# Windowed attention with a gated feed-forward on one core: distance bias on TensorE and a different weave in the first two halves

## The chip, the cores and the metric

The kernel runs on one NeuronCore of a Trainium2 chip. The core has five engines that run side by side, each through its own list of instructions in order: PE (TensorE, matrix multiplies), DVE (VectorE), ACT (ScalarE), POOL (GpSimd) and SP (SyncE, which here only issues DMAs). POOL issues DMAs too. All DMAs share the core's 16 DMA engines. The metric is the device time of one execution in microseconds (us), as the median of several runs; lower is better.

## The reference

Attention over 4 batches, 8 heads, 768 positions and a head width of 64, followed by a feed-forward on the concatenated heads (3072 tokens of width 512, inner width 1536):

```python
scores = scale * np.matmul(q, k.transpose(0, 1, 3, 2))
is_global = pos[None, :] < n_global            # 8 global keys
is_local = (rel >= 0) & (rel < n_local)        # the last 96 keys
dist = np.where(is_global & ~is_local, float(n_local), np.abs(rel))
scores = scores - slopes[:, None, None] * dist[None, :, :]
scores = np.where(is_global | is_local, scores, -1e9)
x = softmax(scores) @ v                        # then heads side by side: 3072 x 512
out = (np.maximum(x @ w_gate, 0.0) * (x @ w_val)) @ w_out
```

All inputs and the output are fp32; the kernel computes in bf16 and accumulates in fp32.

## The kernel before

**Halves.** The work is cut into eight halves s = 0 to 7: half of one batch, 384 query tokens each. Every half has an attention part and a feed-forward part (called c, with the same number). A half's 384 tokens lie on 128 partitions, three tokens each (`NN = 3`).

**Attention of a half.** Heads are handled in four pairs p. Keys are cut into seven tiles of 120 local keys, and the eight global keys are put in front of each tile, so that a tile has 128 rows; only the pieces of the score matrix inside the window are computed. For halves 0 and 1, `piece_cast` turns fp32 q and k of a pair into bf16, `piece_t` transposes them on PE (six 128x128 transposes into PSUM) and copies them out on DVE to `qT` (one copy per head, L259 and L260) and to `kT` (`put_keys`, L238 to L244). For halves 2 to 7 the same is done ahead of time by POOL casts (`kc`, `qz`), DMA transposes on SP (L275, L279) and POOL copies (`early_pieces`); this is called the preparation of a half below. `piece_qk` computes scores for both heads of a pair with one matmul per key tile: the query operand is block-structured, with the other head's 64 rows zero. ACT takes the exponential out of PSUM (L309), and DVE multiplies it by `m_all`, the exponential of the biased distance, which is zero outside the window (L318). `m_all` is made at the start by eight ACT instructions (L209) from the distances `dd`, which POOL and DVE build (L177 to L201). `piece_av` (halves 2 to 7) multiplies by v with a block of ones beside it, so that sums and products come out together; `piece_av_wide` (halves 0 and 1) does sums and products in separate matmuls. ACT then forms the reciprocal as exp(-ln) (`lnd`, `rcp`), and DVE writes the normalised result to `xT` (L351, L377).

**Feed-forward of a half.** `ffn_pieces(c)` gives two lists. f1 has 24 items: for each of 12 slices of 128 inner columns a gate item (four matmuls L408, ReLU on ACT L411) and a val item (four matmuls L418, product on DVE L420 into `ht`). f2 has six items of six matmuls (L427), two for each 128 output rows, then a copy on ACT (L432) and an output DMA on SP (L433). Weights come in three groups of four slices, each group a gate and a val load on POOL's queue (`load_w_group`); `wo_sb` holds the output weights.

**Order.** The order of instructions on each engine is the order in which the Python code issues them. `weave` walks through the feed-forward items and puts attention items between them at given fractions of their total estimated cost. The stages before are:

1. attention of half 0 alone, with loads placed in it by hand (the table `aside`)
2. the first eight items of f1 of half 0, with attention of half 1 spread over them and past their end
3. the first eight items of f1 of half 1
4. the second groups of both halves, with the preparation of half 2
5. the third groups of both halves and both f2 lists, with attention of half 2 and the preparation of half 3
6. then, for c = 2 to 7, f1 and f2 of half c with attention of half c+1 and the preparation of half c+2

The loads of q and k of halves 1 and 2 are held back by `load_qk_after`: DVE writes one element of the target tile, so that the loads, on SP's queue, wait for DVE to get there (L158).

```python
    weave(f1_0[G[0]], spread(attention_pieces(1), 0.1, 1.6),
          [(0.9, lambda: load_w_group(2)), (0.95, lambda: load_w(wo_sb, moe_w_out, 0, DM))])
    ...
    load_qk_after(2)
    load_v_half(2)
    weave(f1_1[G[0]])
    weave(f1_0[G[1]] + f1_1[G[1]], spread(early_pieces(2), 0.0, 1.0),
```

**Buffers.** PSUM has eight banks: three for scores and transposes (`qk_ps`), two for attention output (`av_ps`), three for the feed-forward (`ff_ps`).

Of the kernel before, what the change touches and what calls it, by code (L numbers as in the profile page):

```python
# [8 lines left out]
FP32 = mybir.dt.float32  # L9
# [6 lines left out]
def kernel(  # L16
# [12 lines left out]
    nc = tc.nc  # L29
# [18 lines left out]
    BIG = 1.0e5  # L48
# [13 lines left out]
    banks_of_half[1] = [[by[1, 2], by[1, 5]], [by[1, 3], by[1, 6]], [by[1, 4]]]  # L62

# [4 lines left out]
    es_pool = ctx.enter_context(tc.tile_pool(name="es", bufs=3))  # L68
# [6 lines left out]
    qk_psum = ctx.enter_context(tc.tile_pool(name="qkps", bufs=3, space=bass.MemoryType.PSUM))  # L75
    av_psum = ctx.enter_context(tc.tile_pool(name="avps", bufs=2, space=bass.MemoryType.PSUM))
    ff_psum = ctx.enter_context(tc.tile_pool(name="ffps", bufs=3, space=bass.MemoryType.PSUM))
# [17 lines left out]
    m_all = const.tile([128, H, 2, NN, WQ], BF16)  # L95

# [66 lines left out]
    for p in range(HP):  # L163
        load_qk(0, 2 * p, 2 * p + 2)
    zeros = setupp.tile([128, QH], BF16)
    nc.vector.memset(ident, 0.0)
    nc.vector.memset(zeros, 0.0)
    nc.vector.memset(ones, 1.0)


    dd = setupp.tile([128, 2, NN, WQ], FP32)
    pos = setupp.tile([NG, NN, WQ], FP32)
    relg = setupp.tile([NG, NN, WQ], FP32)
    rel = setupp.tile([128, NN, WQ], FP32)
    sel = setupp.tile([128, NN, WQ], FP32)
    half_w = KT - 0.5
    nc.gpsimd.iota(pos, [[2, NN], [2 * NN, WQ]], base=-(2 * NL + KT - 3), channel_multiplier=0,  # L177
                   allow_small_or_imprecise_dtypes=True)
    nc.gpsimd.iota(relg, [[2, NN], [2 * NN, WQ]], base=-(NL - 1), channel_multiplier=-2,
                   allow_small_or_imprecise_dtypes=True)  # L180
# [8 lines left out]
    nc.gpsimd.affine_select(out=ident, in_=ident, compare_op=ALU.not_equal,  # L189
                            fill=1.0, base=0, pattern=[[-1, 128]],  # L190
                            channel_multiplier=1)
    ga = setupp.tile([NG, NN, WQ], FP32)
    gd = setupp.tile([NG, NN, WQ], FP32)
    nc.vector.tensor_mul(ga, pos, pos)
    nc.vector.tensor_scalar(ga, ga, half_w * half_w, 1.0, op0=ALU.is_gt, op1=ALU.mult)
    nc.vector.tensor_mul(gd, relg, relg)
    nc.vector.tensor_scalar(gd, gd, (NL - 0.5) ** 2, 1.0, op0=ALU.is_lt, op1=ALU.mult)
    nc.vector.scalar_tensor_tensor(out=gd, in0=pos, scalar=half_w, in1=gd,
# [3 lines left out]
    def zero_q(i, p):  # L202
        nc.scalar.copy(qTb[i][64:128, p, 0, :], zeros[64:128])
        nc.scalar.copy(qTb[i][0:64, p, 1, :], zeros[0:64])
# [269 lines left out]
    for i, (_, f) in enumerate(a0):  # L474
        for g in aside.get(i, []):
            g()
# [79 lines left out]
```

The softmax here doesn't subtract the row's maximum and nothing guards it: scores larger than these inputs give would overflow.

## Time and profile before

| what | value |
|---|---|
| median of 5 runs | 258.49 us (257.95 to 260.27) |
| the profiled execution's own time | 260.27 us |
| its span (first to last instruction) | 258.5 us |
| PE busy | 236.5 us (91%) |
| ACT busy | 158.9 us (61%) |
| DVE busy | 139.6 us (54%) |
| POOL busy | 93.0 us (36%) |
| mean granted PE clock | 0.993 |
| first feed-forward matmul begins | 23.69 us |
| last matmul of attention of half 1 | 43.1 us |
| first feed-forward matmul of half 2 begins | 89.8 us |

The span is counted from the first instruction of the profiled execution; 1.77 us of its time lie outside. An engine that is busy for the whole of a stretch sets its length; where no engine is, waits between engines or transfers do. The times of matmuls overlap, so the busy time of PE is read from its start times. Stage boundaries are read from the first start of the matmuls of a stage in the timeline of PE.

### The profile page before, as it was taken

To read this page: it belongs to the slowest core of one execution; us is meant where nothing else is said; L and a number is where in the kernel's file an instruction comes from. 1 tells how busy PE (TensorE), PEld (TensorE's weight loads), DVE (VectorE), ACT (ScalarE), POOL (GpSimd) and SP (SyncE) were. 2 spreads that over 40 slices of the span, in tenths; PEclk is the share of its full clock that TensorE was granted. 3 is DMA by queue.
4 is the path that set the end of the run, shared out by engine and by line. 5 is a ranking of instruction groups with operands and counts; after the bars stand their busy time and mean duration, and the time that the engine had idled before them with its cause. 6 is when DMAs were issued, how large, how long until landed. Compare 5 with 4: busy or idle time off the path is not lost.

```text
span 258.5 us, 4684 instructions
## 1 busy us (share of the span) xinstructions
PE 236.5 (91%) x1599; PEld 138.9 (54%) x1608; DVE 139.6 (54%) x369; ACT 158.9 (61%) x321; POOL 93.0 (36%) x232
## 2 busy tenths in 40 slices
PE   1567698999999999999999999999999999999994
PEld 0335364666555566655665566655565566556641
DVE  7775786464644456534675276625663457614410
ACT  8757277333567577756775577747774677643311
POOL 8951796066544706700644335600640000000000
PEclk9999899999999999999999999999999999999999
DMA  6999699956996994684670984924661200021012
GB/s 181 196 191 234 161 189 205 244 128 144 267 84 176 191 266 112 138 88 148 198 154 13 186 263 104 124 84 144 185 145 42 81 3 0 0 81 43 0 41 82
DMA packets 82695, 34.35 MB, mean 133 GB/s; under 512 B 58608, under 2 KB 79600, under 8 KB 82672
## 3 DMA queue, kind: packets, MB, share of 16 engines
q1 hardware_dynamic: 50816, 26.16, 37.1%
q0 software_dynamic: 31856, 7.91, 31.0%
q8 instruction: 12, 0.20, 0.3%
q14 instruction: 11, 0.09, 0.1%
HBM read 28.38 MB, written 6.29 MB: 134 GB/s over the span
## 4 chain that ended last, share of the span: by engine, by line
PE 79%; DVE 9%; DMA 4%; ACT 4%; issue 1%; SPq 1%; POOL 0%; ACTq 0%; DVEq 0%
PE ff_ps L427 23%; PE ff_ps L418 22%; PE ff_ps L408 22%; PE qk_ps L306 5%; PE av_ps L334 5%; DMA qs<-in_q_dram 4%; DVE xT L351 2%; PE qk_ps L254 1%; DVE ht L420 1%; DVE es L318 1%; ACT lnd L343 1%; DVE qk L223 1%; ACT rcp L348 1%; DVE kT L238 1%; ACT lnd L372 1%
## 5 line engine op out<-in xcount | busy, mean ns | idle before, releaser
L408 PE MATMUL ff_ps<-xT,wg 128*128 128x384 bf16 x384 | 79.0, 328 | 0.4 <-DVE xT L377 0.2
L418 PE MATMUL ff_ps<-xT,wv 128*128 128x384 bf16 x384 | 78.6, 327 | 0.6 <-DVE ht L420 0.3
L411 ACT ACTIVATE grelu<-ff_ps 128x384 bf16<-128x384 f32 x96 | 47.1, 490 | 38.9 <-DVE ht L420 21.8
L420 DVE TENSOR_TENSOR ht<-ff_ps,grelu 128x384 bf16<-128x384 f32 x96 | 53.2, 554 | 28.0 <-PE ff_ps L418 23.6
L427 PE MATMUL ff_ps<-wo_sb,ht 128*128 128x512 bf16 x279 | 66.3, 379 | 0.5
L309 ACT ACTIVATE es<-qk_ps 128x432 bf16<-128x432 f32 (+2 forms) x96 | 49.4, 528 | 19.4 <-PE qk_ps L306 17.3
L318 DVE TENSOR_TENSOR es<-es,m_all 128x432 bf16<-128x432 bf16 (+6 forms) x144 | 42.1, 329 | 23.4 <-ACT es L309 22.9
L351 DVE TENSOR_TENSOR xT<-av_ps,rcp 64x384 bf16<-64x384 f32 x48 | 26.6, 555 | 46.3 <-ACT rcp L348 41.7
L418 PEld LDWEIGHTS <-wv 128*128 128x128 bf16 x384 | 36.6, 98 | 24.4 <-issue 3.4
L408 PEld LDWEIGHTS <-wg 128*128 128x128 bf16 x384 | 36.5, 98 | 23.3 <-issue 0.5
L427 PEld LDWEIGHTS <-ht 128*128 128x128 bf16 x288 | 26.9, 97 | 27.8
L306 PE MATMUL qk_ps<-qT,kT 128*128 128x432 bf16 (+6 forms) x144 | 34.1, 308 | 1.3 <-ACT es L309 1.3
L264 POOL CAST kc<-ks 128x384 bf16<-128x384 f32 x24 | 11.7, 530 | 58.5 <-DMA ks<-in_k_dram 49.0
L343 ACT ACTIVATE lnd<-av_ps 64x384 f32<-64x384 f32 x48 | 23.3, 485 | 11.0 <-PE av_ps L334 10.4
L432 ACT COPY osb<-ff_ps 128x512 f32<-128x512 f32 x24 | 14.1, 586 | 24.4 <-PE ff_ps L427 23.5
L129 POOL DMA_DIRECT2D vbuf<-in_v_dram x28 | 24.4, 878 | 0.8 <-issue 0.4
L334 PEld LDWEIGHTS <-vbuf 128*128 128x128 bf16 x216 | 18.1, 98 | 8.2 <-issue 0.7
L334 PE MATMUL av_ps<-es,vbuf 128*128 128x216 bf16 (+4 forms) x216 | 21.1, 226 | 0.5 <-DVE xT L351 0.5
L306 PEld LDWEIGHTS <-kT 128*128 128x128 bf16 x144 | 14.5, 103 | 12.0 <-issue 3.3
L254 PE MATMUL qk_ps<-ident,qk 128*128 128x128 bf16 x48 | 5.3, 265 | 12.3 <-DVE qk L223 8.3
L272 POOL CAST qz<-qs 128x192 bf16<-128x192 f32 x48 | 14.8, 359 | 2.3 <-DMA qs<-in_q_dram 2.2
L348 ACT ACTIVATE rcp<-lnd 128x384 f32<-128x384 f32 x24 | 12.5, 522 | 0.8
(68 smaller groups left out, 110.5 us busy)
## 6 DMA issues: line engine op xcount, KB each, us to landing
out_dram<-osb SPq DMA_DIRECT2D x24, 256.0 KB
ks<-in_k_dram SPq DMA_DIRECT2D x6, 768.0 KB
qs<-in_q_dram SPq DMA_DIRECT2D x6, 768.0 KB
vbuf<-in_v_dram POOLq DMA_DIRECT2D x24, 120.0 KB, 5.7
ks<-in_k_dram SPq DMA_DIRECT2D x8, 192.0 KB
qs<-in_q_dram SPq DMA_DIRECT2D x8, 192.0 KB
wg<-in_moe_w_gate_dram POOLq DMA_DIRECT2D x3, 512.0 KB, 7.3
wv<-in_moe_w_val_dram POOLq DMA_DIRECT2D x3, 512.0 KB, 9.0
```

The lines of the kernel that those rows point to most:

```text
L129: nc.gpsimd.dma_start(out=v_dst(b, NG + r0, NG + r0 + n, j), in_=v[b, :, KT * j + r0 : KT * j + r0 + n, :].rearrange("h p d -> p h d"))
L306: nc.tensor.matmul(ps[:, c : c + n_], lhsT=kt[:, j, :], rhs=qd[:, :, :, a : a + w], start=True, stop=True)
L309: nc.scalar.activation(es[:, 0:cols], ps[:, 0:cols], AF.Exp, bias=0.0, scale=scale)
L318: nc.vector.tensor_mul(e4, e4, mk)
L334: nc.tensor.matmul(av3[:, :, a : a + w], lhsT=vb[:, j, z0 : z0 + 128], rhs=es[:, c : c + NN * w].rearrange("k (n p) -> k n p", n=NN), star ...
L343: nc.scalar.activation(ln[o0 : o0 + 64], av[d0 : d0 + 64, 0:QH], AF.Ln, bias=0.0, scale=1.0)
L351: nc.vector.tensor_tensor(xT_of[s][r, p, :], av_of[s, p, e_][r, 0:QH], rc[r], op=ALU.mult)
L408: nc.tensor.matmul(psg[:, 0:QH], lhsT=w_of(wg, dc, fc), rhs=xT[:, dc, :], start=(dc == 0), stop=(dc == N_DC - 1))
L411: nc.scalar.activation(gr, psg[:, 0:QH], AF.Relu, bias=0.0, scale=1.0)
L418: nc.tensor.matmul(psv[:, 0:QH], lhsT=w_of(wv, dc, fc), rhs=xT[:, dc, :], start=(dc == 0), stop=(dc == N_DC - 1))
L420: nc.vector.tensor_tensor(ht[:, fc, :], psv[:, 0:QH], st["gr"], op=ALU.mult)
L427: nc.tensor.matmul(ps2, lhsT=ht[:, fc, n * 128 : (n + 1) * 128], rhs=wo_sb[:, fc, :], start=(fc == 0), stop=(fc == N_FC - 1))
```

## The change

In attention of half 0 the window and distance are no longer a factor after the exponential. PE first writes the bias into PSUM (`piece_bias`: a scaled identity `sid` of the head times the distance tile `dd`), then adds the scores (`piece_score`): one matmul per head and key tile that uses only the 64 rows of that head, so that `qT` of half 0 needs no zero blocks and is copied out once. The exponential covers two banks, both heads at once. The PSUM tiles of this part are three of two banks each; they are given back before the feed-forward, which then takes its own (`other_pools`). Transposes move to the `av_ps` banks. `dd` and `BIG` become bf16 values, and the global rows of `dd` are built by POOL instead of DVE.

Seven matmuls on zeros (`warm`) stand at the front of PE's list. The casts of half 0 are spread: pair 0 on DVE, pairs 1 and 2 on ACT, pair 3 on POOL. The eight `m_all` instructions move into the feed-forward that follows. On POOL's queue the loads of v and weights of the first group come after the distances, with the cast of pair 3 between them; the second weight group is issued after the casts of pairs 0 and 1 of half 1, the third after pairs 2 and 3.

The whole f1 list of half 0 (24 items instead of 8) is then woven with attention of half 1, with places given by hand, and half 1 now uses `piece_av`. Then follow f1 of half 1 with the preparation of half 2, and both f2 lists with attention of half 2 and the preparation of half 3. From c = 2 on the order is as before.

```diff
+    first_groups = [[by[0, 0], by[0, 1]], [by[0, 2], by[0, 3]]]
...
-    qk_psum = ctx.enter_context(tc.tile_pool(name="qkps", bufs=3, space=bass.MemoryType.PSUM))
     av_psum = ctx.enter_context(tc.tile_pool(name="avps", bufs=2, space=bass.MemoryType.PSUM))
-    ff_psum = ctx.enter_context(tc.tile_pool(name="ffps", bufs=3, space=bass.MemoryType.PSUM))
+    P["es"] = first.enter_context(tc.tile_pool(name="es2", bufs=4))
+    P["qk"] = first.enter_context(tc.tile_pool(name="qkps2", bufs=3, space=bass.MemoryType.PSUM))
+    def other_pools():
+        first.close()
+        P["es"] = ctx.enter_context(tc.tile_pool(name="es", bufs=3, reuse_waits="tile"))
...
+    nc.vector.memset(wo_sb[:, 0, :], 0.0)
...
+            nc.tensor.matmul(warm_ps, lhsT=wo_sb[:, 0, 0:128], rhs=wo_sb[:, 0, :], start=True, stop=True)
+    warm(7)
...
     for h in range(H):
+        nc.scalar.activation(sid[:, h], ident, AF.Copy, bias=0.0, scale=-slopes[h] / scale)
+
+    def mask(h):
         nc.scalar.activation(m_all[:, h], dd, AF.Exp, bias=0.0, scale=-slopes[h])
...
-            eng = nc.vector if s == 0 else nc.gpsimd
-            eng.tensor_copy(
+            copy = nc.gpsimd.tensor_copy
+            if s == 0 and p < 3:
+                copy = (nc.vector.tensor_copy, nc.scalar.copy, nc.scalar.copy)[p]
...
-        qd = qTb[s % 2][:, p]
-        nc.vector.tensor_copy(qd[0:64, 0, :], tp[0:64, 0, :])
-        nc.vector.tensor_copy(qd[64:128, 1, :], tp[64:128, 0, :])
+        if s == 0:
+            nc.vector.tensor_copy(qTb[0][:, p, 0, :], tp[:, 0, :])
...
+    def piece_bias(p, g):
+        ps = P["qk"].tile([128, 2, 512], FP32, name="qk_ps")
...
+                nc.tensor.matmul(ps[:, e, c : c + NN * w], lhsT=sid[:, 2 * p + e],
+                                 rhs=dd[:, 0 if j == 0 else 1, :, m : m + w],
+                                 start=(i == 0), stop=False, skip_group_check=True)
...
+    def piece_score(p, g):
...
+                r = slice(64 * e, 64 * e + 64)
+                nc.tensor.matmul(ps[:, e, c : c + NN * w], lhsT=kt[r, j, :],
+                                 rhs=qd[r, :, a : a + w], start=False, stop=(i == len(group) - 1),
+                                 skip_group_check=True)
...
+        nc.scalar.activation(es, ps[:, :, 0:cols], AF.Exp, bias=0.0, scale=scale)
...
         if s == 0:
-            return (C(0) + T(0) + C(1) + T(1) + QK(0) + C(2) + T(2) + QK(1) + C(3) + T(3) + QK(2) + AW(0)
-                    + QK(3) + AW(1) + AW(2) + AW(3))
+            return (C(0) + X(lambda: load_v_globals(0), lambda: load_v(0, 0)) + C(3)
+                    + X(lambda: load_v(0, 1), lambda: load_v(0, 2), lambda: spread_v_globals(0, 1, 4),
+                        lambda: load_v(0, 3), lambda: load_w_group(0))
+                    + C(1) + T(0) + BI(0, 0, 1) + C(2) + T(1) + SC(0, 0, 1) + BI(1, 0) + SC(1, 0) + T(2)
+                    + BI(1, 1) + SC(1, 1) + BI(2, 0) + T(3) + SC(2, 0) + BI(2, 1) + SC(2, 1)
+                    + BI(3, 0) + SC(3, 0) + BI(3, 1) + SC(3, 1)
+                    + AW(0) + X(lambda: load_qk_after(1, True)) + AW(1) + AW(2) + AW(3) + X(other_pools))
         if s == 1:
...
+            return ([(0.0, lambda: C_(0)), (0.0, lambda: C_(1)), (0.02, lambda: load_w_group(1)),
+                     (0.04, lambda: C_(2)), (0.05, lambda: C_(3)), (0.07, lambda: load_w_group(2))]
+                    + [(0.08, lambda j=j: fill_ones(nc.gpsimd, 0, j)) for j in range(NT)]
+                    + [(t, lambda p=p: piece_t(1, p)) for p, t in enumerate((0.10, 0.14, 0.20, 0.26))]
...
-    weave(f1_0[G[0]], spread(attention_pieces(1), 0.1, 1.6),
-          [(0.9, lambda: load_w_group(2)), (0.95, lambda: load_w(wo_sb, moe_w_out, 0, DM))])
+    weave(f1_0, attention_pieces(1),
+          [(0.05 * h, lambda h=h: mask(h)) for h in range(H)])
...
+    load_w(wo_sb, moe_w_out, 0, DM)
...
-    weave(f1_1[G[0]])
-    weave(f1_0[G[1]] + f1_1[G[1]], spread(early_pieces(2), 0.0, 1.0),
-          [(0.1 + 0.12 * j, lambda j=j: fill_ones(nc.vector, 0, j)) for j in range(NT)])
+    weave(f1_1, spread(early_pieces(2), 0.0, 1.0))
...
-    weave(f1_0[G[2]] + f1_1[G[2]] + f2_0 + f2_1,
-          spread(attention_pieces(2), 0.3, 0.9), spread(early_pieces(3), 0.4, 0.8))
+    weave(f2_0 + f2_1, spread(attention_pieces(2), 0.0, 0.9), spread(early_pieces(3), 0.2, 0.7))
```

## The prediction

> **What bounds the kernel now.** I read the span in slices first, then the stretches between the stage boundaries, the waits of PE, and the queues of POOL and SP.
>
> ```profile
> PE   1567698999999999999999999999999999999994
> POOL 8951796066544706700644335600640000000000
> DMA  6999699956996994684670984924661200021012
> ...
> PE 79%; DVE 9%; DMA 4%; ACT 4%; issue 1%; SPq 1%; POOL 0%; ACTq 0%; DVEq 0%
> ```
>
> One slice is 6.46 us. From the eighth on PE is at its limit; only the first seven, 43 us, have room. The stretches, cut at the stage boundaries (columns: stretch and length; busy time and count of PE, weight loads, DVE, ACT, POOL; granted clock; DMA share; GB/s):
>
> ```profile
> 0.00:23.69 23.69, 11.16 (x104) 7.11 (x105) 16.91 (x63) 18.02 (x37) 15.85 (x36) 1.00 1.33 197
> 23.69:43.06 19.37, 15.52 (x160) 9.39 (x157) 14.46 (x48) 11.55 (x25) 15.65 (x33) 0.91 1.01 189
> 43.06:89.98 46.92, 46.08 (x281) 26.23 (x282) 23.05 (x54) 24.13 (x50) 22.22 (x56) 1.00 1.00 177
> 89.98:118.45 28.47, 28.32 (x192) 16.93 (x192) 15.74 (x41) 19.65 (x39) 9.95 (x27) 1.00 0.77 151
> ```
>
> By 43.06 only eight f1 items are done (four matmuls each start 0.65 us apart as a group: 5.2 us) besides two attentions. From 43.06 on PE is 98% busy. So a gain can come only from the first two rows, and what counts is when c = 2 begins, 89.98; the remaining 168.5 us I leave as they are. Why PE starves there:
>
> ```profile
> PE qk_ps L254 <- DVE qk L223: 8.3, 3, 4.3
> PE qk_ps L254 <- POOL qk L223: 2.3, 1, 2.3
> ...
> 24.49 0.51 POOL L223 CAST qk<-qs 128x384 bf16<-128x384 f32 x1 [1.30 <-DMA qs<-in_q_dram]
> ...
> 28.28 0.51 POOL L223 CAST qk<-qs 128x384 bf16<-128x384 f32 x1 [1.10 <-DMA qs<-in_q_dram]
> ```
>
> In half 0 transposes wait for DVE's casts, since DVE does casts, copies and mask products in one row (transposes at 4.33, 7.36, 11.50, 15.45). In half 1 they wait for q and k from memory. A third loss follows from the second (rows as above):
>
> ```profile
> 26.46:29.87 3.41, 1.12 (x12) 0.77 (x12) 1.54 (x7) 0.49 (x1) 2.10 (x5) 1.00 0.67 210
> 29.87:33.28 3.41, 3.41 (x14) 1.73 (x13) 3.00 (x10) 1.94 (x4) 3.41 (x9) 0.50 0.68 90
> 19.63:23.04 3.41, 2.08 (x43) 1.66 (x42) 2.33 (x7) 3.08 (x8) 0.35 (x1) 1.00 1.19 231
> ```
>
> After 3.41 us in which PE was busy for 1.12, the clock is halved for 3.41 us, which loses 1.7 us of work; after 2.08 it was not.
>
> **What the Trainium skill says.** "TensorE: Matmul & The Clock Gate" (Part 1: The HAM clock gate) describes this: full clock after about 3.4 us of work, half after such an idle window. The trace agrees (six transposes take 0.82 us until 15.45, 0.50 from 25.40). The same page (Part 3: Packing small matmuls) says matmuls on separate row groups run side by side; no run here shows it. "DMA: Bandwidth & Descriptors" (Issuing engines are not separate DMA queues) says transfers of all issuers share 16 engines and interleave. The trace agrees with weights (19 to 22 us: 0.42 MB from POOL's queue, 0.27 MB from SP's), not with v: q and k of half 2, issued at 43.92, moved nothing to speak of until 48, while v moved (45.5 to 47.5: 0.30 MB, all POOL's).
>
> **Step 1, half 0.** Casts of pair 0 ran at 3.63 and 3.91, close behind their data, so the first transposes stay at 4.3. DVE loses ga/gd (2.6 us), six casts, 16 mask products (4 us) and one copy per pair; per pair it keeps 0.35 + 0.53 + 0.17 + 0.18 = 1.25 us. ACT takes over: eight `sid` (about 0.2 each, shorter than the 0.49 of 384 columns), four casts (0.49), then per pair exponentials of 864 and 336 columns: by the 0.0008 us per column between 384 and 512 columns, 0.89 + 0.45 = 1.34. ACT can start them after its casts, 7.4, and ends at about 13.8; then 4 x (0.49 + 0.52) for ln and exp. POOL's distance chain ends near 5.0 instead of 2.8, so v globals and tile 0 are issued by 6.9, the cast of pair 3 (its data arrive at about 8) runs until 8.8, and v tiles 1 to 3 are issued by 11.6; alone on the engines they need about 3.7 us from issue to landing (5.7 before, beside q and k): 14.6. That is the wait that replaces DVE's: the products of pair 0 wait for it, with the rest of PE's list behind. xT of pair 0 is done at 15.7 and, at ACT's 1.01 us per pair, of pair 3 at 19.05. Gate 0 ends at 19.7, against 24.9.
> Not shown before: 32 bias matmuls, 4 x 1200 columns, 0.5 us per pair at full clock, 1.0 at half. Bounds: below zero no, since they only add work; 0 behind ACT's 1.34 per pair, 2 us if the clock stays low. I take 0. Scores in row halves: 0.5 (side by side) or 1.0 per pair, both under 1.34: 0. Seven warming matmuls of 0.43 lie in the wait before 4.3: 0 to +0.3; their gain is contained in "full clock by about 8"; without it up to 1.7 us are lost.
>
> **Step 2, transfers.** The first weight group is issued at 11.6 instead of 7.76; 0.5 MB takes 2.6 us alone (landings at 35.0 and 37.6 before). wg lands at 18, wv, sharing with q and k of half 1, at 21.2. q and k (issued 15.75; before 15.45) are no longer beside the second group: alone they move at 350 GB/s, 0.6 us per transfer. Pair 0 is cast at 23.0, pair 1 at 24.7, pair 2 at 27.2, pair 3 at 28.2; transposes at 23.1, 24.8, 27.3, 29.2 (before 25.4 to 36.5). With val 0 waiting for wv until 21.2, eight items and all transposes are done at 30.4. The second group is now behind two casts on POOL, 24.7 instead of 14.87: it lands at 31.2 and 33.1, so gate 4 waits 0.7 and val 4 1.05. The third is issued at 28.2, lands by 38.5 and is needed at 40: hidden. `wo_sb` moves from 32.0 to 35.4, behind seven memsets more (2 us) on POOL: hidden, as f2 is far.
>
> **Step 3, the weave.** Left on PE at 30.4: 16 items x 0.65 = 10.4, eight score groups x 0.2 = 1.6, eight products x 0.3 = 2.4, waits 1.75: 46.5. From 25.3 ACT has 19.6 us (12 exponentials, five masks, ten ReLUs, eight ln, four exp), DVE from 25.5 18.9 us: until 45. Three engines almost full lose something to each other; I take 1.0 (0 to 3.5). f1 of half 0 ends at 47.5. Before, the same work was done at 43.06 + 10.4 = 53.5.
>
> **Step 4, preparation of half 2.** f1 of half 1: 15.6 + 0.3 for the last xT; the first f2 item ends at 64.7. Next on PE are scores of half 2. Their q and k are released by DVE at the end of f1 of half 0, 48.7.
>
> ```profile
> 43.92 0.37 SPq L110 DMA_DIRECT2D ks<-in_k_dram  x1
> 44.34 0.65 SPq L110 DMA_DIRECT2D qs<-in_q_dram  x1
> 46.80 6.17 SPq L125 DMA_DIRECT2D vbuf<-vbuf  x6
> 54.35 4.72 SPq L275 DMA_TRANSPOSE kN<-kc  x3
> 59.24 3.94 SPq L279 DMA_TRANSPOSE qT<-qz  x3
> ```
>
> Before, 43.92 to the landing of the last transpose, about 64.5, was 20.6 us, covered by 23.5 us until the first scores at 67.47. Now the cover is 16. From the k data on, the chain is 12 us (POOL 1.9, SP 4.7 + 3.9, landing 1.3) and stays. Only the data can be quicker: 4.1 us of the 20.6 were v tiles ahead; `wo_sb` now ends near 46, v near 50, so about 1.3 to 2 us of waiting remain. Ready at 65.9; PE waits 1.2.
>
> **Step 5.** Rest of f2: 11 x 1.3 = 14.3, attention of half 2 4.9, waits 0.4 as before: c = 2 begins at 85.5. The preparation of half 3 ends near 84.3, just ahead. 89.98 - 85.5 = 4.5 us. Against the profiled execution's 260.27 (span 258.5 and 1.77 around it) that is 255.8; its time is 1.78 above the median, so against the median 258.49 it is 254.0.
>
> **Rivals.** **A, main:** 254.0, own range 252.5 to 256.5, chance 0.50. **B, fewer waits:** weights and half 2 arrive just in time, no loss between engines: f1 ends at 45.0, half 2 without a wait: 7.7 us, 250.8. For it: DMA had idle time at 28 to 30. Against: four transfers are issued late. Chance 0.17. **C, ACT and DVE bound the weave:** 19.6 us of ACT work in 22 us, in fixed order: f1 ends at 50, 256.5. For it: the masks moved there. Chance 0.20. That the change does not do what it says, the clock staying low through half 0, costs 1 to 1.7 us and falls here. **D, slower: half 2 is late.** q and k of half 2 wait 6 us behind `wo_sb` and v (4.1 before), ready at 71.3: PE stands 6.6 us instead of 1.2 and the clock is halved after it, 1.7 more: 7.1 us worse than A, 261.1. It decides from 5.7 us of wait and clock together. For it: SP and POOL do this chain one after the other. Against: wo's issue moves by 3.4 us only. Chance 0.13.
>
> **The numbers.** A measurement of this kernel can tell about 0.5% from no change, 1.3 us: faster is below 257.2. Of A nearly all (0.48), B, and two thirds of C (0.13): 0.78; rests of A and C and the mild end of D: 0.10; D: 0.12. Range 250.5 to 259.5: it reaches from B to the near side of D and leaves out most of D and a better B.
>
> **What would show it.** First gate near 19; transposes of half 1 between 23 and 30; a wait of gate 4 for weights; c = 2 near 85.5; PE idle before the first scores of half 2 for 0 to 3 us. Wrong: a wait there above 5 us, a halved clock after 20, or f1 of half 0 ending after 51.

## The result and the profile after

The changed kernel takes 259.83 us (median of 43 runs, 258.89 to 262.28), the kernel before 258.83 (80 runs, 257.55 to 261.67) beside it. The ratio is 1.0037 (95% interval 1.0024 to 1.005): no gain, but a loss of 0.2 to 0.5%. The forecast was 254.0, with 0.78 on faster. The profiled execution took 259.35 us, its span is 257.6.

Beside the span in slices of 6.44 us stands the chain of work that ended last; this is the page of the kernel after:

```profile
PE   7744988999898899999999999999999999999994
PEclk9996799999999999999999999999999999999999
DMA  6999999994899993855682985937581200021012
...
PE 66%; DMA 16%; DVE 5%; ACT 4%; SPq 4%; POOL 2%; issue 2%; DVEq 0%; ACTq 0%; POOLq 0%
```

The first two slices are fuller than before (77 for 15), the third and fourth emptier (44 for 67), and the fourth and fifth ran at a low clock. In the chain the share of PE fell from 79% to 66% and that of DMA rose from 4% to 16%: the end is now reached by way of transfers. The stretches of the kernel after, cut at the last `xT` of half 0, the end of f1 of half 0, the begin of f2 and the last matmul of the first gate of c = 2 (columns as in the prediction):

```profile
0.00:19.65 19.65, 12.66 (x159) 7.92 (x159) 8.31 (x31) 13.54 (x29) 15.93 (x38) 1.00 1.01 150
19.65:50.02 30.37, 25.06 (x180) 15.79 (x181) 18.96 (x57) 20.73 (x44) 19.76 (x43) 0.89 1.31 199
50.02:66.28 16.26, 15.99 (x98) 9.38 (x97) 7.80 (x17) 5.89 (x13) 6.73 (x22) 1.00 0.87 174
66.28:89.59 23.31, 20.75 (x121) 10.67 (x123) 10.78 (x25) 14.50 (x31) 15.23 (x35) 1.00 1.20 212
```

Half 0 is done at 19.65, some 4 us earlier than before. Then 30.4 us pass until f1 of half 0 ends, where the forecast had 28.4 (19.05 to 47.5). What PE waits for there, in the timeline of PE of the kernel after (start, length, instruction, and in brackets the idle time ahead of it and what ended it):

```profile
20.25 0.82 PE L478 MATMUL ff_ps<-xT,wg 128*128 128x384 bf16 x4 [2.98 <-DMA wg<-in_moe_w_gate_dram]
23.79 1.46 PE L488 MATMUL ff_ps<-xT,wv 128*128 128x384 bf16 x4 [2.71 <-DMA wv<-in_moe_w_val_dram]
35.71 0.82 PE L488 MATMUL ff_ps<-xT,wv 128*128 128x384 bf16 x4 [1.23 <-DMA wv<-in_moe_w_val_dram]
68.36 0.53 PE L355 MATMUL qk_ps<-qT,kT 128*128 128x432 bf16 x2 [0.63 <-DMA qT<-qz]
81.36 0.42 PE L383 MATMUL av_ps<-es,vbuf 128*128 128x216 bf16 x4 [0.96 <-DVE xT L400]
89.59 0.32 PE L478 MATMUL ff_ps<-xT,wg 128*128 128x384 bf16 x1 [0.77 <-DVE xT L400]
```

Gate 0, val 0 and val 4 (the first val item on the second weight group) all wait for weights. Why these are late is in POOL's queue and in what the DMA engines moved meanwhile. POOL in the kernel after:

```profile
8.13 0.50 POOL L236 CAST qk<-ks 128x384 bf16<-128x384 f32 x1 [1.17 <-DMA ks<-in_k_dram]
9.23 2.70 POOL L141 DMA_DIRECT2D vbuf<-in_v_dram  x3
11.92 0.79 POOL L158 DMA_DIRECT2D wg<-in_moe_w_gate_dram  x1
24.36 0.51 POOL L236 CAST qk<-qs 128x384 bf16<-128x384 f32 x1 [0.66 <-DMA qs<-in_q_dram]
26.70 0.79 POOL L158 DMA_DIRECT2D wg<-in_moe_w_gate_dram  x1
```

The transfers between 8 and 16 us, in slices of 0.2 us, first of the kernel before and then of the kernel after:

```profile
DMA  9999999999999999999999999999999999999999
...
DMA packets 5099, 1.50 MB, mean 187 GB/s; under 512 B 4098, under 2 KB 5099, under 8 KB 5099
```

```profile
DMA  9999920000001012999999999999999999989999
...
DMA packets 4611, 0.76 MB, mean 96 GB/s; under 512 B 4379, under 2 KB 4610, under 8 KB 4610
```

The cast of pair 3 waits at the head of POOL's queue for its k, the v loads and the first weights stand behind it, and from 9.2 to 11.2 the DMA engines have next to nothing to do. Between 8 and 16 us the kernel after moves 0.74 MB less. At the roughly 190 GB/s at which the kernel before was moving, that is 3.9 us of transfers (an estimate), and from 11.2 on the transfers fill the engines without a gap until the second weight group has landed. So the debt stays, and by this estimate it is as long as the lead of half 0.

One thing about the reference has to be known for the comparison. The execution that the prediction read had a stretch of halved clock in the weave of half 1. A second execution of the same kernel before (`b_again`, 259.05 us, span 257.3) has none, and there c = 2 begins at 88.62, not 89.82. The stretch that was at half clock, and the first gate of c = 2, in that second execution:

```profile
29.87:33.28 3.41, 3.41 (x30) 2.25 (x28) 3.40 (x11) 2.65 (x6) 3.41 (x10) 1.00 0.61 85
...
88.62 0.81 PE L408 MATMUL ff_ps<-xT,wg 128*128 128x384 bf16 x4
```

So 1.2 us of the loss that the prediction set out to recover are not there in most executions: of the 43 runs of the kernel before beside `b_again`, 11 had a mean clock of 0.991 to 0.993 and took 259.92 us or more; of the 32 with 0.997 to 1.0 all but one (259.85) took 259.25 or less.

### The profile page after: what moved, and what is told of

It reads as the page before. It is cut to its first block, busy times and chain, and to the rows that moved or that the text cites. A ratio compares the mean times of both kernels' runs of the same rounds, so it can differ in the third digit from the quotient of the medians.

```text
span 257.6 us, 4673 instructions
## 1 busy us (share of the span) xinstructions
PE 237.8 (92%) x1614; PEld 139.7 (54%) x1623; DVE 130.7 (51%) x333; ACT 159.3 (62%) x325; POOL 97.1 (38%) x244
## 4 chain that ended last, share of the span: by engine, by line
PE 66%; DMA 16%; DVE 5%; ACT 4%; SPq 4%; POOL 2%; issue 2%; DVEq 0%; ACTq 0%; POOLq 0%
PE ff_ps L497 20%; PE ff_ps L488 18%; PE ff_ps L478 18%; PE av_ps L383 5%; DMA qs<-in_q_dram 5%; PE qk_ps L355 4%; DVE xT L400 3%; DMA wv<-in_moe_w_val_dram 3%; DMA out_dram<-osb 3%; DMA ks<-in_k_dram 2%; SPq L122 2%; DMA vbuf<-in_v_dram 2%; DVE ht L490 2%; SPq L291 1%; ACT lnd L392 1%
## 5 line engine op out<-in xcount | busy, mean ns | idle before, releaser
L481 ACT ACTIVATE grelu<-ff_ps 128x384 bf16<-128x384 f32 x96 | 47.0, 490 | 38.1 <-DVE ht L490 18.2
L400 DVE TENSOR_TENSOR xT<-av_ps,rcp 64x384 bf16<-64x384 f32 x56 | 31.1, 555 | 47.0 <-ACT rcp L397 38.7
L358 ACT ACTIVATE es<-qk_ps 128x432 bf16<-128x432 f32 (+2 forms) x84 | 44.2, 532 | 13.8 <-PE qk_ps L355 12.3
L367 DVE TENSOR_TENSOR es<-es,m_all 128x432 bf16<-128x432 bf16 (+6 forms) x128 | 38.1, 328 | 26.8 <-ACT es L358 26.2
L392 ACT ACTIVATE lnd<-av_ps 64x384 f32<-64x384 f32 x56 | 27.2, 485 | 12.8 <-PE av_ps L383 12.0
L355 PE MATMUL qk_ps<-qT,kT 128*128 128x432 bf16 (+6 forms) x128 | 28.8, 285 | 0.7 <-DMA qT<-qz 0.6
L383 PEld LDWEIGHTS <-vbuf 128*128 128x128 bf16 x256 | 21.0, 98 | 10.8 <-issue 2.7
L383 PE MATMUL av_ps<-es,vbuf 128*128 128x216 bf16 (+5 forms) x256 | 24.8, 225 | 1.7 <-DVE xT L400 1.7
L355 PEld LDWEIGHTS <-kT 128*128 128x128 bf16 x128 | 12.3, 98 | 10.4 <-issue 2.2
L397 ACT ACTIVATE rcp<-lnd 128x384 f32<-128x384 f32 x28 | 14.6, 522 | 0.9
L251 POOL COPY kT<-kN 128x360 bf16<-128x360 bf16 x12 | 6.5, 541 | 6.9 <-DMA kN<-kc 6.9
```

Source lines behind the costliest of these rows:

```text
L355: nc.tensor.matmul(ps[:, c : c + n_], lhsT=kt[:, j, :], rhs=qd[:, :, :, a : a + w], start=True, stop=True)
L358: nc.scalar.activation(es[:, 0:cols], ps[:, 0:cols], AF.Exp, bias=0.0, scale=scale)
L367: nc.vector.tensor_mul(e4, e4, mk)
L383: nc.tensor.matmul(av3[:, :, a : a + w], lhsT=vb[:, j, z0 : z0 + 128], rhs=es[:, c : c + NN * w].rearrange("k (n p) -> k n p", n=NN), star ...
L392: nc.scalar.activation(ln[o0 : o0 + 64], av[d0 : d0 + 64, 0:QH], AF.Ln, bias=0.0, scale=1.0)
L400: nc.vector.tensor_tensor(xT_of[s][r, p, :], av_of[s, p, e_][r, 0:QH], rc[r], op=ALU.mult)
```

## The experiments

All are ratios to the kernel before, run in turns with it on the same chip. The theory after the result was that transfers set the end of the first weave. The rivals were the clock of PE, the attention chain on ACT and DVE, and a fault of the new half 0 or of the new weave alone. `b_again` above was the first run.

> The kernel before, unchanged, for a second profile. The profiled execution shown so far took 260.27 us, 1.4 above the median of its runs, while that of the changed kernel was 0.5 below the median of its own. If the spread is the clock: an execution near 258.8 us shows no halved clock in the weave of half 1 (29.87 to 33.28 us in the first profile) and begins c = 2 about 1.5 us earlier, near 88.3. If it is transfers: the halved stretch is there again, and q and k of half 1 arrive earlier.

### Is it the halved clock?

In the kernel after the clock is halved from 21.88 to 28.70. Its first 3.4 us:

```profile
21.88:25.29 3.41, 1.50 (x5) 0.74 (x6) 0.00 (x0) 0.63 (x2) 1.01 (x2) 0.50 1.38 247
```

`e1_fill` fills the two weight waits with matmuls on zeros:

```diff
-                    + AW(0) + ... + AW(3) + X(other_pools))
+                    + AW(0) + ... + AW(3) + X(other_pools, lambda: fill_gap(8)))
...
-            return ([(0.0, lambda: C_(0)),
+            return ([(0.0, lambda: fill_gap(12)), (0.0, lambda: C_(0)),
```

> The changed kernel with 20 more matmuls on zeros (8 after the last product of half 0, 12 after gate 0), so that PE stays busy while it waits for weights and the clock is not halved from 21.9 to 28.7 us. Clock theory: half of the 4.9 us that PE worked in that stretch comes back, 2.0 to 2.5 us faster than the changed kernel (257.5 to 258). Transfer theory: the transposes of half 1 come up to 1 us earlier, but val 4 still starts when its weights land at 35.7, so within 0.6 us of the changed kernel.

Measured: 260.49 us, ratio 1.0036 (1.0014 to 1.0058), the same as the kernel after. The profile has full clock throughout, and yet val 4 waits as before:

```profile
34.59 0.82 PE L493 MATMUL ff_ps<-xT,wv 128*128 128x384 bf16 x4 [1.04 <-DMA wv<-in_moe_w_val_dram]
```

This execution (258.67 us) is one of the faster ones of this kernel, but the others show the same: those with a mean clock of 0.997 to 1.0 took 258.67 to 261.19 us, the rest 258.34 to 261.74. What PE gained by the clock it lost again to waits, for weights and for the casts of half 1: as long as transfers bound the weave, the clock is not the cause.

### Is it the gap in the transfers?

`e2_cast3` takes the waiting cast away from POOL and gives it to DVE, behind the copies of pair 1; nothing else is touched:

```diff
-            if s == 0 and p < 3:
-                copy = (nc.vector.tensor_copy, nc.scalar.copy, nc.scalar.copy)[p]
+            if s == 0:
+                copy = (nc.vector.tensor_copy, nc.scalar.copy, nc.scalar.copy, nc.vector.tensor_copy)[p]
...
-            return (C(0) + X(lambda: load_v_globals(0), lambda: load_v(0, 0)) + C(3)
+            return (C(0) + X(lambda: load_v_globals(0), lambda: load_v(0, 0))
...
-                    + ... + C(2) + T(1) + SC(0, 0, 1) + ...
+                    + ... + C(2) + T(1) + C(3) + SC(0, 0, 1) + ...
```

> The changed kernel with the cast of pair 3 of half 0 on DVE, after the copies of pair 1, so that POOL issues v tiles 1 to 3 and the first weights without waiting for q and k of pair 3. v tile 3 and the weights are issued about 2.2 us earlier (wg at 9.7). Transfer theory: no wait for v in half 0 (1.4 us before), gate 0 near 19, val 0 near 21.7, and 1.0 to 2.0 us faster than the changed kernel. If q, k and the second weight group set the end of the weave alone: within 0.6 us of the changed kernel.

Measured: 258.13 us, ratio 0.9956 (0.9937 to 0.9974), 0.8% faster than the kernel after by the two ratios. The first gate weights are issued at 9.90 instead of 11.92, 1.13 MB are moved between 8 and 16 us instead of 0.76, and val 4 starts at 33.52. A new wait appeared, since now the copies of the global v rows are late:

```profile
16.23 0.25 PE L418 MATMUL av_ps<-es,vbuf 128*64 128x144 bf16 x2 [1.50 <-DMA vbuf<-vbuf]
```

`e4_globals` removes that one by loading these rows first of all:

```diff
     warm(7)
+    load_v_globals(0)
...
-            return (C(0) + X(lambda: load_v_globals(0), lambda: load_v(0, 0))
+            return (C(0) + X(lambda: load_v(0, 0))
```

> The kernel with the cast of pair 3 on VectorE, and besides the load of the v rows that serve as globals issued first of all on POOL's queue, ahead of the distance chain (it stood behind cast 0). Transfer theory: the wait of the first products for the spread v rows (2.5, 1.5 in the run without this move) goes, half 0 ends about 1.5 earlier, the first gate weights still land by then, and the kernel is 0.5 to 1.5 us faster than the kernel with the cast alone (258.13): about 257. Rival (the end of the weave of half 1 is set by q, k of half 1 and the second weight group alone): the 1.5 us turn into a longer wait for q, k or for the second group, 258 as before.

Measured: 257.6 us, ratio 0.9943 (0.992 to 0.9966). The wait is gone and gate 0 begins at 17.54, but against `e2_cast3` the two ratios differ by 0.13%, which is inside their intervals: a further gain is not shown. In the profiles f2 begins 0.5 us earlier, and the first scores of half 2 then wait longer for their preparation (1.42 us for 0.68). Val 4 in `e4_globals`:

```profile
32.98 0.82 PE L489 MATMUL ff_ps<-xT,wv 128*128 128x384 bf16 x4 [1.08 <-DMA wv<-in_moe_w_val_dram]
```

This instruction turned out to be the hinge. From its start to the begin of f2 it is 30.57 us in the kernel after (35.71 to 66.28), and 30.57 to 30.59 in `e1_fill`, `e2_cast3`, `e4_globals`, `e6_weave_alone` and `e7_qk1_early`: in these kernels PE works from there to f2 without a wait that differs, so up to f2 only the start of val 4 counts. And where it waits for its weights, it starts when much the same bytes have been moved since the start: 6.39 MB by 35.71 in the kernel after, 6.37 by 34.59 in `e1_fill`, 6.30 by 33.52 in `e2_cast3`, 6.30 by 32.98 in `e4_globals`. More of them were moved early in the last two (1.13 and 1.20 MB between 8 and 16 us, for 0.76).

Closing the first gap opened a second one, though. The second weight group stands on POOL's queue behind the casts of pairs 0 and 1 of half 1, and those wait for q and k. In `e4_globals` only 0.15 MB moved from 24.5 to 26.5, when q and k had nearly all landed and the group was just being issued (1.14 MB moved in the 3.5 us ahead of that). `e2_cast3` has the same gap. POOL in `e4_globals`:

```profile
23.92 0.51 POOL L237 CAST qk<-qs 128x384 bf16<-128x384 f32 x1
24.38 0.79 POOL L158 DMA_DIRECT2D wg<-in_moe_w_gate_dram  x1
```

So it is not the sum of bytes alone that sets val 4, but the chain of transfers, casts and the issue behind them.

### Order of the transfers

`e3_w1first` issues the second weight group ahead of the casts of half 1, `e7_qk1_early` is `e4_globals` with q, k of half 1 released some 4 us earlier:

```diff
-            return ([(0.0, lambda: C_(0)), (0.0, lambda: C_(1)), (0.02, lambda: load_w_group(1)),
+            return ([(0.0, lambda: load_w_group(1)), (0.0, lambda: C_(0)), (0.0, lambda: C_(1)),
```

```diff
-                    + ... + T(3) + SC(2, 0) + ... + AW(0) + X(lambda: load_qk_after(1, True)) + AW(1) + ...
+                    + ... + T(3) + X(lambda: load_qk_after(1, True)) + SC(2, 0) + ... + AW(0) + AW(1) + ...
```

> The changed kernel with the second weight group issued on POOL ahead of the casts of half 1 instead of behind two pairs of them (near 19 instead of 26.7 us). Transfer theory: it lands about 3 us earlier, val 4 does not wait, the casts of half 1 come 1 to 2 us later; 0.5 to 1.5 us faster than the changed kernel. If sharing costs q and k more than this: the transposes come over 3 us later, and it is up to 1.5 us slower.

> The kernel of e4_globals with the release of the q, k loads of half 1 moved ahead, from behind the first products to behind the transposes of pair 3, so that VectorE reaches it near 12 instead of 16.2. Transfer theory: q, k land by 24 to 25 instead of 28.5, the transposes of half 1 run at 20 to 25, the second weight group is issued 2 to 3 us earlier and no longer waited for, and the first feed-forward of half 0 ends near 45 instead of 50.0: 254 to 256. Rival (the transfers only change places: q, k delay the first gate and value weights by as much as they gain): within 1 us of e4_globals.

Measured: 261.83 (ratio 1.0101, 1.006 to 1.0142) and 257.85 us (0.9955, 0.9936 to 0.9973). In the first the second group comes in time, but the last transposes of half 1 wait for their q and k; in the second q and k come in time, but val 0 and val 4 wait for weights. The lines of `e3_w1first` and then of `e7_qk1_early`:

```profile
33.01 0.51 PE L267 MATMUL av_ps<-ident,qk 128*128 128x128 bf16 x6 [2.18 <-POOL qk L236]
```

```profile
21.95 0.82 PE L489 MATMUL ff_ps<-xT,wv 128*128 128x384 bf16 x4 [2.62 <-DMA wv<-in_moe_w_val_dram]
...
34.79 0.82 PE L489 MATMUL ff_ps<-xT,wv 128*128 128x384 bf16 x4 [2.36 <-DMA wv<-in_moe_w_val_dram]
```

My expectation for `e7_qk1_early` missed: I had again priced a transfer as if it were alone. In this kernel the engines have no gap between 16 and 36 us, q and k moved at some 245 GB/s beside the weights and v where in `e4_globals` they had reached 330, and the second group was issued at 24.71, no earlier than the 24.38 there. Bringing this transfer forward pushed others back.

### Half 0 and weave apart

`e6_weave_alone` is half 0 of the kernel before with the weave and the stages of the kernel after:

```diff
...
-    weave(f1_0[G[0]], spread(attention_pieces(1), 0.1, 1.6),
-          [(0.9, lambda: load_w_group(2)), (0.95, lambda: load_w(wo_sb, moe_w_out, 0, DM))])
+    weave(f1_0, attention_pieces(1))
...
-    weave(f1_1[G[0]])
-    weave(f1_0[G[1]] + f1_1[G[1]], spread(early_pieces(2), 0.0, 1.0), ...)
+    weave(f1_1, spread(early_pieces(2), 0.0, 1.0))
```

> Half 0 of the kernel before with the weave and the stages of the kernel after (the whole first feed-forward of half 0 with attention 1, the second weight group behind two casts, the output weights later). Transfer theory: q, k of half 1 are issued as early as before, so the weave finds them in time; the end of the first feed-forward of half 0 comes near 49.5 and the time is 257 to 259. Rival (the new weave itself costs): 260 to 262.

Measured: 257.87 us, ratio 0.9947 (0.9928 to 0.9967), as the transfer theory had it. The stretches of this kernel from its first gate to the end of f1 of half 0 and then to f2, and val 4; then the stretch that answers to the first, in `e4_globals`:

```profile
23.97:48.00 24.03, 22.80 (x184) 14.64 (x181) 19.20 (x58) 17.93 (x37) 16.79 (x38) 1.00 1.26 172
48.00:64.20 16.20, 15.93 (x97) 9.38 (x96) 7.75 (x17) 5.85 (x12) 6.48 (x21) 1.00 0.80 159
...
33.62 0.81 PE L428 MATMUL ff_ps<-xT,wv 128*128 128x384 bf16 x4
```

```profile
17.54:47.40 29.86, 24.73 (x185) 15.49 (x182) 20.67 (x59) 22.16 (x47) 19.65 (x43) 0.94 1.24 195
```

This is the clearest pair. `e4_globals` enters the weave 6.4 us earlier (17.54 for 23.97), and the weave takes 5.8 us longer (29.86 for 24.03), with val 4 at 32.98 for 33.62. Two kernels whose halves 0 are 6.4 us apart differ by 0.6 at f2, and by 0.3 us in the time, which is inside the intervals. In `e6_weave_alone` PE is busy for 22.80 of the 24.03 us and val 4 does not wait; in `e4_globals` PE stands for 5 us of the 29.86, and 3.4 of the rest are at half clock. The traces show why a shorter half 0 brought so little: the inputs of half 1 were not asked for earlier along with it: q and k are issued from 15.73 in the one and from 16.60 in the other, the second weight group at 23.01 and 24.38. The new weave gains by itself about 1 us (0.5%); the new half 0 adds nothing to it that can be told from the noise, and as it stands in the kernel after, with the gap in its transfers, it takes away about 2.

The other half of this, the new half 0 with the old stages, I tried twice (`e5_first_alone`, `c5_first_alone`). In the second the ones beside v are filled behind the third cast of half 1; in it and in the next three kernels plain DMA copies of the same bytes stand in place of the DMA transposes of halves 2 to 7, so that the transposing is left out.

```diff
+    load_w_group(1)
+    for j in range(NT):
+        fill_ones(nc.gpsimd, 0, j)
...
+    weave(f1_0[G[0]], spread(attention_pieces(1), 0.1, 1.6),
+          [(0.9, lambda: load_w_group(2)), (0.95, lambda: load_w(wo_sb, moe_w_out, 0, DM))])
```

> Half 0 of the kernel after (bias on TensorE, scores in row halves, PE kept busy) with the stages behind it of the kernel before (a third of the first feed-forward woven with attention 1, the second weight group issued ahead of that weave). Transfer theory: half 0 finishes 2 us earlier than before, but q, k of half 1 are issued 0.8 later than before and the second weight group stands ahead of the casts, so the transposes of half 1 come no earlier than before and the gain is lost in the weave: 258.5 to 261. Rival (half 0 carries a gain and the new weave loses it): 254 to 256.

> e5_first_alone with the fills of the v buffers' ones moved from the head of POOL's queue to behind the third cast of half 1, where their wait for the spread v rows holds up no transposes of pair 0 (that wait of 13.2 at 33.83 was an effect of where I had put them, and hid the answer); DMA transposes replaced by copies. Transfer theory: the gain of half 0 is lost to the second weight group and q, k of half 1, which come no earlier than before: 258 to 261. Rival (half 0 carries a gain that the new weave loses): 254 to 256.

Measured: 276.65 us (ratio 1.0683, 1.0631 to 1.0734) and 268.79 (1.0379, 1.0329 to 1.0428). Neither theory had that. As in the kernel after, half 1 uses `piece_av` here, which needs blocks of ones in the v buffers, and filling them stood in POOL's way both times; here the first:

```profile
33.83 2.01 POOL L146 MEMSET vbuf<- 128x288 uint32 x7 [13.24 <-DMA vbuf<-vbuf]
35.80 0.49 POOL L236 CAST qk<-ks 128x384 bf16<-128x384 f32 x1
```

All casts of half 1 stood behind a wait of 13.2 us. In the second POOL still waited 3.1 us ahead of the fills, with the last casts behind them, and the clock was halved for 27 of the first 60 us. What the new half 0 is worth with the old stages is therefore not settled by these two.

### Transfers taken away

`c0_after_copy` is the base (the kernel after, with copies for transposes). `c9_no_qk1` leaves out the load of q and k of half 1 besides and takes the rows of half 0 for them, and `c8_v1_late` is `e4_globals` with copies for transposes, the v rows of half 1 behind the second weight group and the products of half 1 placed later:

```diff
+    def same_qk(s):
+        qs_of[s], ks_of[s] = qs_of[0], ks_of[0]
...
-                    + AW(0) + X(lambda: load_qk_after(1, True)) + AW(1) + ...
+                    + AW(0) + AW(1) + ...
...
+            same_qk(1)
```

```diff
-    load_v_half(1)
...
+            ... (0.02, lambda: load_w_group(1)), (0.03, lambda: load_v_half(1)),
```

> The kernel after, with the 36 DMA transposes of q, k of halves 2 to 7 replaced by plain DMA copies of the same bytes (the transposing is left out; everything up to the begin of f1_1 is untouched). It is the base for the next three, which have the same replacement. Both theories: val 4 waits for its weights and f2 begins near 66.3 as in the kernel after; behind that, copies that take less than the transposes would take away the 0.6 that the first scores of half 2 wait: 258.5 to 260.

> The kernel after, without the load of q, k of half 1: half 1 takes the f32 rows of half 0 in their place, so 1.5 MB of transfers and the wait for them are left out, and all instructions on the engines stay; DMA transposes replaced by copies. Transfer theory: the casts of half 1 run at once, the second weight group is issued near 18 to 20 instead of 26.7 and lands by 28 to 29 instead of 35.7, f2 begins near 60 instead of 66.28: 252 to 254. Rival (PE, its halved clock or the chain of attention 1 sets the weave): f2 begins at 65 or later, 257 to 259.

> e4_globals with the v rows of half 1 loaded behind the second weight group instead of ahead of q, k of half 1, the products of half 1 placed some 0.08 of the weave later, and DMA transposes replaced by copies. In every kernel with the new weave f2 began 30.57 to 30.59 after the first value matmul on the second weight group, so the landing of that group sets the time. Transfer theory (what stands ahead of that group in the transfers sets it): without the three v tiles (some 2.7 us of transfer) ahead, it lands near 30 instead of 33.0, f2 begins near 61 instead of 63.56, and the time is 255 to 256. Rival (the products, later and behind a late v, become the bound): f2 begins no earlier than 63, 257 to 258.5.

Measured, as ratios to before: base 257.93 us, 0.9942 (0.992 to 0.9963); without q, k 255.21 us, 0.9807 (0.9755 to 0.9859); v late 256.24 us, 0.9888 (0.9857 to 0.992). Val 4 and the begin of f2 in the base, and then in `c9_no_qk1`:

```profile
36.71 0.82 PE L489 MATMUL ff_ps<-xT,wv 128*128 128x384 bf16 x4 [1.22 <-DMA wv<-in_moe_w_val_dram]
...
67.28 1.46 PE L498 MATMUL ff_ps<-wo_sb,ht 128*128 128x512 bf16 x6
```

```profile
32.69 0.81 PE L493 MATMUL ff_ps<-xT,wv 128*128 128x384 bf16 x4
...
63.85 1.46 PE L502 MATMUL ff_ps<-wo_sb,ht 128*128 128x512 bf16 x6
```

With 1.5 MB less to move, and the work of the engines in place but for the two one-element writes that held these loads back, the wait of val 4 is gone and f2 begins 3.4 us earlier (the second group was issued at 21.12 for 27.71). That is the transfer theory, in this execution at about half the size I had expected. What is left of the weave is in its line:

```profile
20.15:47.70 27.55, 24.47 (x181) 15.39 (x182) 19.30 (x59) 20.81 (x45) 18.69 (x42) 0.94 1.34 166
```

The first weights are still waited for, a product waits 1.30 for `xT`, and the clock is halved from 22.6 to 26.0. With the transfers out of the way the clock does seem to count: two of the six runs, both with a mean clock of 0.993, took 252.2 and 252.3 us, inside the 252 to 254 that I had expected, and the four with 0.977 to 0.987 took 255.0 to 255.7. No profile was taken of the two. The run does not separate the bytes of q and k from the wait of the casts for them, since both went. And the base begins val 4 and f2 a microsecond later than the kernel after (36.71 for 35.71, 67.28 for 66.28), though up to val 4 they have the same instructions, so single profiles of this stretch differ by that much.

That f2 now begins at 63.85, where the prediction had 63.4, points to the transfers of q and k as what it had mispriced; that the two numbers are so close is in part luck, with the clock halved in the one and not in the other.

`c8_v1_late` missed. F2 began at 65.28 and not near 61: q and k, with no v ahead, met the first weights (val 0 waited 2.23), the later casts stood behind the three v issues on POOL (a wait of 1.07 at 29.54), and the products, placed later, waited for `xT` (0.41 to 0.62 each). It is 1.7 us faster than the base, no more than `e4_globals` is against the kernel after (2.2), so the edit itself shows no gain.

The base itself, at 257.93 a little faster than expected, answers a question on f2, with the stretch from the begin of f2 to the first gate of c = 2:

```profile
67.28:88.85 21.57, 20.59 (x125) 10.76 (x123) 9.86 (x25) 14.61 (x31) 14.29 (x32) 1.00 1.19 222
```

21.57 against 23.31 us in the kernel after: with the transposes replaced, the wait of 0.63 is gone. `c9_no_qk1` has 21.57 too, while the kernels with transposes take 23.31 to 24.21 (`e1_fill` and `e4_globals`). That the wait of 0.96 has shrunk to 0.22 need not be the copies' doing: it is 0.22 in `e1_fill` and `e6_weave_alone` as well, which have the transposes.

Of the complete kernels `e4_globals` has the lowest ratio: 0.57% faster than the kernel before (interval 0.34 to 0.80), and 0.9% faster than the kernel after by the two ratios. `e2_cast3`, `e6_weave_alone` and `e7_qk1_early` cannot be told from it.

## Why the prediction was wrong

It was wrong: 259.83 against 254.0, outside the range. The difference is 5.8 us, and it splits by the prediction's own milestones.

- **Reference, 1.2 us.** Its third loss (a halved clock after a window with 1.12 us of PE work) was in the execution it was read from, and not in the second one. I had seen the execution to be 1.78 above the median, and subtracted that as an offset, while still counting its cause among the gains. One of the two had to go. What differs between the two executions can be read off: the clock rises at 19.6 in the first and at about 20.8 in the second, where the time of eight equal matmuls falls from 0.71 to 0.45 us between 19.90 and 21.20. Counted on from there in steps of 3.41 us, the second one's windows begin at 24.25 and 27.66 and hold 2.15 and 2.30 us of work. The first execution, then two lines and two windows of the second:

```profile
19.80 0.45 PE L366 MATMUL av_ps<-es,ones 128*64 128x216 bf16 x8
```

```profile
19.90 0.71 PE L366 MATMUL av_ps<-es,ones 128*64 128x216 bf16 x8
...
21.20 0.45 PE L366 MATMUL av_ps<-es,ones 128*64 128x216 bf16 x8
...
24.25:27.66 3.41, 2.15 (x17) 1.11 (x14) 2.23 (x7) 0.98 (x2) 1.02 (x2) 1.00 1.14 291
27.66:31.07 3.41, 2.30 (x20) 1.60 (x21) 1.75 (x7) 0.90 (x2) 2.87 (x6) 1.00 0.39 117
```

- **Step 2, transfers, 2.9 us: the step that failed.** It said of q and k: "alone they move at 350 GB/s, 0.6 us per transfer", and from this had pair 1 cast at 24.7 and the second group issued at 24.7, landed at 33.1. The price is right where they are alone: in `e6_weave_alone` 1.27 MB, most of it q and k, moved at 363 GB/s between 18.5 and 22. Here they were not alone. They were issued from 16.27 (15.75 forecast), but until 20.3 only POOL's queue moved anything. All transfers of the kernel after between 16.5 and 20.3:

```profile
DMA packets 687, 0.62 MB, mean 162 GB/s; under 512 B 89, under 2 KB 687, under 8 KB 687
...
q0 software_dynamic: 687, 0.62, 115.0%
```

  Then q and k shared the engines with the v tiles of half 1 until 28. The step had only taken the second weight group away from their side; the first group, 4 us later than before, and those v tiles had come to it. The last cast of pair 1 ran at 26.25, the group was issued at 26.70, val 4 began at 35.71 for 33.1: 2.6 of the 2.9. The first weights were misjudged in the same way: landed at 18 and 21.2 by the forecast, 20.25 and 23.8 in the trace. The sum that was missing is that of bytes: step 1 wrote down that v is issued by 11.6 and weights behind it, and did not ask what the DMA engines do in the meantime. The delay at the start was in the prediction's own trace: q and k of half 1 were issued there from 15.45 and moved no packet until 18.2, and of q and k of half 2 the prediction itself wrote that they "moved nothing to speak of until 48" while v moved. Step 2 put nothing in for it.
- **Steps 4 and 5, f2, 1.2 us.** The wait for the preparation of half 2 was priced at 1.2 and measured 0.63: right in mechanism. "Waits 0.4 as before" was too little: a product of attention 2 waits 0.96 and the first gate of c = 2 waits 0.77. These two and the 0.63 are 0.8 more than the 1.6 that was forecast; the other 0.4 is spread over work and small waits. That attention 2 now lies within f2 alone may be the reason; no run tests it.
- **The rest, 0.5 us.** The profiled execution of the kernel after is 0.5 below its median. (The kernel before, too, has a median 0.34 higher over its 80 runs than over the five that the forecast started from.)

**What held.** Step 1: first transposes at 4.40 (4.3 forecast), the end of the exponentials at 13.95 (13.8), a wait of the first products for v of 1.4 in two parts, last `xT` at 19.65 (19.05). The hit on the exponentials is in part luck: 7.4 and four times 1.34 make 12.8 and not 13.8; they took 1.22 per pair, began at 7.94 and waited 1.13 us for scores on the way. Likewise 15.7 and three times 1.01 make 18.7 for the last `xT`. The bias matmuls add no wait that shows on ACT's path beyond that one. The third group and `wo_sb` are hidden. Behind c = 2 nothing moved: from the last matmul of its first gate to the end of the span it is 168.0 us in the kernel after, and about 168.2 in both executions of the kernel before. (The 89.98 of the prediction is a matmul late; the gate begins at 89.82.)

**Rivals.** C had f1 of half 0 end at 50, and it did (50.02), but not for its reason, so that this is luck: without q and k to load the same ACT and DVE work fitted 27.55 us. B's own terms make 8.2 us and not 7.7 (2.5 for f1 and 1.2 for half 2, on top of 4.5); it changes nothing here. D, a late half 2, was 0.63 us instead of 6.6. The rival that was missing is the one that came true: POOL's loads wait, and the transfers become the bound of the weave. Of the signs that were to show it wrong one came true and one nearly: the clock was halved after 20, though `e1_fill` shows that this alone cost nothing that can be measured, and f1 of half 0 ended at 50.02, for 51.

The page of the Trainium skill that the prediction cited on shared engines ("DMA: Bandwidth & Descriptors", Issuing engines are not separate DMA queues) was the right one, and the cited sentence already forbids the price "alone". The same page (Queues, rings and completion order) says that each engine takes turns between the queues it has work for, packet by packet; from 20.5 on that fits, with 2177 packets of SP's queue beside 2044 of POOL's until 28. In the 4 us before it the trace shows no turns at all, and no run here tells why. The kernel before has such a stretch as well, from 15.45 to 18.2.

## What to carry over

Where transfers fill the engines, count bytes by a deadline, not the duration of one transfer: a stage that was made 6 us shorter, while the inputs of the next one were asked for no earlier and had the same bytes ahead of them, bought 6 us of waiting. An instruction that waits at the head of a queue that also issues loads costs DMA time; here one cast and a 2 us gap were worth about 2 us at the end, and with that gap closed another opened behind the next casts. Before a loss in a profile is counted as recoverable, look at whether a second execution has it.

## What the runs showed of the hardware

- Loads on SP's queue, issued while loads on POOL's queue were in flight, began late, and by different amounts: 4.0 us in the kernel after (issued from 16.27, no packet until 20.3), 4.0 in `e7_qk1_early`, 2.8 in the kernel before, 2.2 in `e4_globals`, 1.0 in `e2_cast3`. What sets the delay stays open.
- Whether the clock is halved goes with the work in windows of 3.41 us whose beginning differs between executions of one kernel. Counted back and forth from the halved stretches of eleven profiles (the kernels before and after, `e2_cast3`, `e3_w1first`, `e4_globals`, `e5_first_alone`, `e7_qk1_early` and the four with copies), all 15 windows at full clock with 1.32 us of PE work or less (0.64 to 1.32) were followed by half clock, none with 1.96 or more was, and between 1.75 and 1.94 both occurred (in the kernel before from 19.6 on, where it is at full clock). In the second execution of the kernel before the stretch from 26.46 to 29.87 holds 1.29 us and no halving follows; by the working above it is not a window there.
- Scores in row halves take less time than as many full-height matmuls, which no run had shown when the prediction was made. In the kernel after four bias matmuls on 128 rows take 0.47 us from their start to the next start, and four score matmuls of as many columns, on 64 rows each, half of them on the one row half and half on the other, take 0.30:

```profile
11.84 0.54 PE L320 MATMUL qk_ps<-dd,sid 128*128 128x216 bf16 x4
12.31 0.36 PE L337 MATMUL qk_ps<-qT,kT 64*128 64x216 bf16 x4
12.61 0.34 PE L320 MATMUL qk_ps<-dd,sid 128*128 128x144 bf16 x4
```

- With DMA transposes the stretch of f2 took 23.31 to 24.21 us, with copies of the same bytes 21.57 in two kernels and 22.28 in `c8_v1_late`.
